# A longer written emission order, finer filler matmuls and re-measured plan durations in a linear-attention and mixture-of-experts kernel

## The chip, the cores and the metric

One core of one Trainium2 chip. The metric is the device time of one execution in microseconds (us); lower is better. The engines are PE (TensorE: matmuls, with PEld for its weight loads), DVE (VectorE), ACT (ScalarE), POOL (GpSimd) and SP (SyncE), which here only issues DMAs. Each engine works through its own instructions in the order in which the program was written; engines wait for one another through semaphores.

## What is computed

A linear attention over 8 batches, 8 heads, 576 positions and 64 dimensions, whose result goes as x (4608 rows of 512) into a dense mixture of 8 experts with Sinkhorn-normalised routing weights P.

```python
def phi(x):
    return np.where(x > 0, x, np.exp(x) - 1.0) + 1.0
kv  = einsum('bhsd,bhse->bhde', phi(k), v);  z = phi(k).sum(axis=2)
x   = einsum('bhsd,bhde->bhse', phi(q), kv) / (phi(q) @ z + 1e-06)   # (N, 512), N = 4608
logits = x @ w_gate;  P = exp(logits - logits.max())                  # (N, 8)
for _ in range(8):
    P /= P.sum(1, keepdims=True) + 1e-09
    P /= P.sum(0, keepdims=True) + 1e-09
    P *= N / E
for e in range(8):
    out += P[:, e:e+1] * (np.maximum(x @ w1[e], 0) @ w2[e])           # w1: 512x1024, w2: 1024x512
```

## The kernel before

**Stages.** In the front, the attention runs in 16 groups (8 batches by two groups of four heads), written by `att` (line 319). A group loads k, q and v; makes phi(k) with an exp on ACT and two passes on DVE (`f_e`, `f_t`, `f_m`); accumulates kv and z on PE (`f_kv`, line 366) and evicts them into a block-diagonal tile (`f_z`); transposes q on PE (`f_qt`) and makes phi(q) (`f_qe` on ACT, `f_qm` and `f_qp` on DVE); multiplies by z (`f_den`, two halves), takes the reciprocal on ACT as exp(-ln) (`f_ln`, `f_ex`); multiplies by kv (`f_num`, two halves) and writes the quotient into xT on DVE (`f_x`). All of q's, den's and the logits' results share two PSUM banks (`at2`), kv and num share one.

The experts go over nine row groups g of 512 rows each, a pair of expert and group being a unit, numbered 9e + g. Expert 0 runs beside the front and behind it: its first five groups plainly (`layer1`, line 600, four matmuls of 512 columns per block of hidden units, evicted by relu on ACT or DVE, then `f_y`, line 847, layer 2), the last four with seven products instead of eight per 2x2 block (`block7`, line 701). From unit 9 on, `unit` (line 926) does both layers with seven products: for layer 1 the products m1 to m7 of two halves a and b (`pm`, 4 matmuls of 256 columns each, evicted by `f_seed`, `f_s2`, `f_s5`, `f_h11`, `f_h21` on ACT and `f_h12`, `f_h22` on DVE), for layer 2 the products y1 to y7 (8 matmuls each). The sums of weights that these need are made on DVE once per expert, W from w1 and T from w2 (`combos`, four instructions each); the sums of h once per unit, S (`f_S`, line 933, four instructions). A product of layer 2 is scaled by P and added to acc on DVE (`f_e`, line 982, two per product), except y2, which goes over ACT (`f_a`) and POOL (`f_g`). Groups 0 to 7 of expert 0 are finished before P is known: their layer 2 is copied to acc (`f_fin`) and scaled later in place, 32 instructions of `f_s` (line 876), on DVE or ACT.

**Who sets the order.** Every piece of work is a task with an engine (or a choice of two), a planned duration, its dependencies and the buffers that it takes. `_Plan.run` (line 54) emits the tasks one by one. First it takes those of a written list, `_FRONT`, number and engine letter (p PE, a ACT, d DVE, g POOL, s SP, m a DMA's landing, n none), 993 of them, which ends on PE with unit 9's y6. From there on it always emits the task that the plan can start first, the smaller `prio` first where several can. From unit 8 on the order on PE is also a fixed chain:

```python
    order = "y1 y5 y2 a7 y6 y3 a4 b1 b5 y7 b6 b3 b2 b7 A1 A5 y4 b4 A6 A3 A2".split()
```

In a unit's stretch y stands for layer 2 of the unit before, a and b for its own layer 1, A for the next unit's half a. Each such stretch is 112 matmuls of 256 columns.

**Filler.** At the start PE has nothing to do; `f_warm` (line 537) multiplies zero tiles into a bank that nobody reads, 47 matmuls of 512 columns in 34 tasks, each put behind the one before and held by its own earliest time (`after`).

**Loads.** All loads of q, k, v and of the weights (which convert to 16 bits) are issued on POOL, in order, at most eight in flight; the first k goes over SP. Expert e's w1 comes in two halves, w2 in one piece (in quarters and halves for expert 0). From unit 9 on x is read back from DRAM per unit, on SP (`x_load`), where `x_blocks` stored it before.

Of the kernel before, what the change touches and what calls it, by code (L numbers as in the profile page):

```python
# [17 lines left out]
class _Plan:  # L18
# [119 lines left out]
    1n 2p 3p 4p 5p 6p 7p 36s 37m 8p 43d 42a 105n 94n 571n 38g 39m 0g 40g 41m 63g 64m 44d 65g 66m 67g 68m 112g 113m  # L138
    45n 9p 10p 49n 50p 114g 115m 11p 12p 51a 139g 140m 76n 46p 52d 13p 47a 14p 95g 96m 97g 98m 53d 15p 48d 141g 142m
    16p 69a 70d 17p 54p 18p 116g 117m 55a 19p 20p 71d 100g 101m 77p 72n 73p 21p 78a 79d 22p 23p 24p 56p 74a 75d 25p  # L140
    118a 80d 143g 144m 26p 57a 119d 59p 27p 102g 103m 81p 58a 28p 120d 29p 30p 166g 167m 31p 32p 82a 60d 99n 83p 106g
    107m 168g 169m 61p 62d 84a 33p 34p 125n 35p 85a 126p 86p 146d 572p 573p 127a 87d 128d 574p 88p 170g 171m 575p
    121n 109g 110m 152n 89d 145a 153p 147d 193g 194m 154a 122p 576p 129d 123a 578p 580p 155d 156d 197g 198m 124a 104n
    148n 130p 579d 577a 581d 131a 195g 196m 90g 91m 149p 132p 582p 133a 584p 150d 151d 173d 222g 223m 583a 134a 586p
    585d 137p 157p 588p 108n 138d 158a 587d 135p 172a 159p 179n 592p 590p 160a 161a 608n 92g 93m 136d 251g 252m 180p
    174d 175n 176p 181a 591d 594p 177d 589a 111n 182d 178a 249g 250m 593p 183d 162p 226g 227m 184p 595p 600a 163d
    185a 200d 253g 254m 199a 164p 186p 165d 596p 206n 609p 187a 602d 224g 225m 201d 229d 188a 305g 306m 207p 280g
    281m 202n 203p 208a 611p 204a 610d 228a 209d 210d 613p 598p 612a 278g 279m 614d 205a 211p 191p 212a 597p 213p
    192d 604d 189p 214a 615p 230d 190d 215a 220p 216p 256d 221a 599p 235n 616d 217d 255a 231n 257d 236p 237a 238d
    617p 606a 218p 311a 619p 262n 263p 219d 618a 258n 239d 232p 309g 310m 264a 233d 234d 629p 265d 621p 620a 307g  # L150
    308m 240p 259p 282g 283m 241a 260d 622a 623p 261a 266d 242p 332g 333m 243a 244a 336g 337m 624d 642p 245p 285d
    267p 641n 644p 643d 246d 268a 627p 312d 645a 269p 270a 271a 247p 291n 630p 359g 360m 248d 334g 335m 536d 292p
    313d 274p 284a 646p 275d 648p 286d 293a 272p 287n 294d 647a 628p 318n 273d 314n 361g 362m 365a 319p 537d 635d
    320a 288p 390g 391m 295d 289d 650p 290a 338a 631p 321d 296p 315p 649d 339d 297a 298p 651d 299a 652p 654p 322d
    388g 389m 316d 317d 300a 653d 303p 323p 655a 304d 632p 324a 637d 301p 366d 325p 326a 327a 656p 625p 363g 364m
    345n 302d 543d 328p 346p 657d 626p 329d 340d 347a 471g 472m 341n 330p 639a 674n 442g 443m 675p 348d 372n 331d
    367d 373p 349d 342p 374a 368n 538d 677p 469g 470m 392g 393m 343a 676a 344a 375d 660p 394a 376d 417g 418m 395d
    396d 539s 540m 350p 661p 351a 633d 679p 668a 352p 355p 353a 664p 354a 665p 544d 276p 356d 357p 358d 277a 401n
    419g 420m 402p 415g 416m 369p 545d 403a 678d 546s 547m 473g 474m 370a 658p 659p 371a 404d 377p 680a 397n 681p
    683p 666a 378a 478g 422d 526n 682d 684d 421a 379p 382p 662p 380a 381a 383d 685p 663p 687p 550d 686a 551d 448a  # L160
    423d 444g 445m 384p 689p 688a 428n 385d 429p 475a 707n 690a 405d 398p 708p 430a 431d 399a 710p 400a 406p 709a
    449d 424n 552d 553s 554m 425p 407a 555s 556m 432d 408p 426a 446g 447m 541s 542m 712p 427d 409a 711a 713d 411p
    386p 410a 714p 670d 387a 433p 412d 476d 691p 527g 528m 529g 530m 434a 450d 672a 715a 413p 414d 477d 435p 436a
    437a 716p 717d 455n 718p 548s 549m 438p 456p 557d 457a 693p 479n 439d 440p 719d 458d 694p 451n 441d 564d 565d
    459d 483n 484p 485a 452p 453a 532n 533g 534m 486d 692p 699a 720p 454d 701a 460p 461a 480p 462p 487d 481a 482d
    463a 558d 722p 467p 695p 464a 488p 468d 696p 489a 566d 465p 490p 491a 492a 466d 721a 703d 723d 697p 698p 705a
    493p 724p 494d 725p 495p 732a 730p 496d 728p 731p 738a 524n 751n 744d 745d 497p 746d 740d 747s 748m 525p 498a
    729p 741d 742d 743d 752p 796d 766p 753a 499d 754p 756p 755a 726p 957s 958m 1014s 1015m 757a 797d 758p 760p 767a
    772p 759a 773a 762p 761d 770p 500p 763d 768p 798d 764p 749s 750m 799s 800m 776p 501d 502d 765a 769a 727p 771a
    803n 804p 805a 774p 806p 808p 736a 777d 807a 810p 775d 778p 809a 535n 811a 734d 812p 503p 786p 779a 818p 813d  # L170
    504d 848d 787p 505d 849d 784p 819a 824p 794a 825a 820p 814p 821a 815d 782p 506p 828p 559d 783p 829d 816p 850d
    560s 561m 826p 507d 817a 562s 563m 790a 827d 785p 822p 792a 508d 856p 830p 823a 780p 857a 900d 781p 855n 509p
    831a 510d 834p 567s 568m 511d 835p 860p 788a 801s 802m 870p 862p 901d 836p 863a 861a 871a 842d 512p 858p 513d
    837p 859a 872p 844a 864p 514d 873a 876p 851s 852m 877a 866p 853s 854m 874p 902d 838p 867d 569s 570m 875a 903s
    904m 839p 865d 846d 878p 868p 879d 832p 869a 905s 906m 531n 515p 880p 908p 833p 909a 881d 910p 516d 911a 907n
    517d 890p 912p 882p 891p 883a 840a 914p 913a 915a 898a 922p 923a 518p 916p 884p 917d 918p 519d 919d 949d 950d
    926p 924p 925a 951d 886p 952d 928p 920p 929a 921a 885p 927a 930p 932p 960p 933d 961a 962p 892a 520d 887p 934p
    966p 948n 963a 888p 889p 967a 953d 935a 931d 896a 959n 968p 964p 965a 970p 521p 971d 936p 969d 972p 974p 976p
    522d 523d 975a 937p 977a 980p 981a 894d 973a 944a 954d 955d 982p 978p 984p 1017p 985d 1019p 986p 979a 603d 942p
    943p 706d 983d 1071s 1072m 1018a 1020a 987a 1023p 947a 988d 989d 1024a 895d 605d 940p 941p 956d 938p 601d 946d  # L180
    1025p 939p 945a 990d 1021p 992p 993a 994p 997p 1027p 669d 1016n 991d 607d 634d 1002p 1000a 996d 1022a 995d 1028d
    1001g
# [4 lines left out]
def kernel(  # L187
# [10 lines left out]
    nc = tc.nc  # L198
# [6 lines left out]
    P = 128  # L205
    PW = 64
    NJ = S // PW
    NG = N // 512
# [110 lines left out]
    def att(b, g):  # L319
# [5 lines left out]
        for nm, ten in (("k", k), ("q", q), ("v", v)):  # L325
# [15 lines left out]
            ti = fadd(("sp", 0.45) if sp else ("pool", 0.73), fn, acq=[gr, *gsw], use=gsw, prio=pr)  # L341
            tin[nm] = fadd(("dma", 1.47 if nm == "k" else 1.42), lambda _: None, deps=[ti], use=[gr, *gsw], prio=pr, lat=2.15)
# [38 lines left out]
        for r in range(2):  # L381
            def f_z(e, r=r):
                s = slice(64 * r, 64 * r + 64)
                src = gkv["tile"][s, :, 64 * r:64 * r + 2 * D].rearrange("p h (z d) -> p h z d", z=2)
                dst = gz["tile"][s, :, :, 64 * r:64 * r + 64]
                copy(e, dst, src if r == 0 else src[:, :, ::-1])
            tz.append(fadd({"dve": 0.40, "act": 0.42}, f_z, deps=[tkv, *tz], use=[gkv, gz], prio=pr))
# [70 lines left out]
    def logits(b2):  # L458
# [11 lines left out]
        t1 = lg_pe[b2] = add(("pe", 1.0), f_l, deps=wg_done + [xt_done[(b, c)] for b in (2 * b2, 2 * b2 + 1) for c in range(NDT)],  # L470
# [4 lines left out]
    def sinkhorn():  # L475
# [10 lines left out]
        for it in range(8):  # L486
# [27 lines left out]
            a = add(("dve", 2.6), f_a, deps=last, prio=-200.0)  # L514
            c = add(("pe", 0.2), f_c, deps=[a], acq=[gc], prio=-200.0, lat=0.15)
            last = [add(("dve", 0.45), f_d, deps=[c], use=[gc], prio=-200.0)]
# [18 lines left out]
    t_id[0] = add(("pool", 1.5), f_init, prio=-290.0)  # L535

    def f_warm(_, n=1):
        for _ in range(n):
            nc.tensor.matmul(yw[0], lhsT=warm[:, 0:P], rhs=warm, start=True, stop=True)
# [6 lines left out]
    for i in range(34):  # L546
        twa = add(("pe", 0.3), lambda e, n=2 if 4 <= i < 17 else 1: f_warm(e, n), deps=[twa], use=[gyw], prio=900.0, after=1.2 + 0.5 * i)
# [93 lines left out]
    def x_blocks(g):  # L641
# [10 lines left out]
        for i in range(3):  # L652
# [16 lines left out]
            last = add(("dve", 0.8 if i == 0 else 0.42), f_T,  # L669
# [8 lines left out]
        def f_st(_):  # L678
            nc.sync.dma_start(out=xd[g][:, 1536:NXB], in_=gt_["tile"].rearrange("p i c t -> p (i c t)"))
        ti = add(("sp", 0.45), f_st, deps=[last], use=[gt_], prio=0.0)  # L680
        out_ = [add(("dma", 1.5), lambda _: None, deps=[ti], use=[gt_], prio=0.0, lat=2.6)]
        ti = add(("sp", 0.9), f_raw, deps=deps + [ti], prio=0.0)
        out_.append(add(("dma", 1.0), lambda _: None, deps=[ti], prio=0.0, lat=2.6))
        x_users.append(out_[1])
        if early:
# [415 lines left out]
```

## Time and profile before

| | us |
|---|---|
| median of 3 runs (lowest, highest) | 970.96 (970.43, 971.53) |
| profiled execution | 971.46 |
| its span, first to last instruction | 969.7 |
| PE busy in it | 956.1 |
| DVE, ACT, POOL busy | 769.4, 572.1, 144.1 |
| granted TensorE clock, mean | 0.999 |
| first zero matmul starts | 1.33 |
| first transposes, first kv, first den start | 6.91, 9.37, 12.38 |
| first expert matmul starts | 21.76 |
| first layer-2 product of units 9, 10, 11, 12 | 199.06, 212.13, 226.72, 238.94 |

The parts of the page are read so: busy time of each engine; the same in 40 slices; DMA queues; the chain of work that ended last; the costliest groups of instructions, each with its line, shapes, count, busy time and the idle time before it, with what ended that idle time; the DMA issues. A matmul's end is modelled and includes its drain, so that matmuls that follow each other overlap in the record: the distance of their starts is what one costs.

### The profile page before, as it was taken

The numbers are of one execution on the slowest core, as the hardware profiler recorded it, in microseconds if no ns is written. First come the engines' busy times: TensorE is split into PE (matmuls) and PEld (weight loads), VectorE is DVE, ScalarE is ACT, GpSimd is POOL, SyncE is SP. The second block draws the span as 40 slices with busy tenths as digits, with TensorE's granted clock in tenths as the row PEclk, the third lists the DMA queues.
The fourth block names the chain that finished last, engine by engine and source line by source line (L and its number), as shares of the span: only waits on it lengthen the run. The fifth ranks groups of instructions, "written<-read, shape, count | busy, mean of one in ns | idle before, by whom it ended". The sixth has DMA issues, their size and how long they took to land.

```text
span 969.7 us, 21145 instructions
## 1 busy us (share of the span) xinstructions
PE 956.1 (99%) x8625; PEld 795.5 (82%) x8625; DVE 769.4 (79%) x1469; ACT 572.1 (59%) x1016; POOL 144.1 (15%) x209
## 2 busy tenths in 40 slices
PE   8999999999999999999999999999999999999998
PEld 4555566678888888888888888888888888888886
DVE  6887888797887888878887888878887888877775
ACT  6787864575555555555555555555555555555553
POOL 6422100020112111111112111111112111111110
PEclk9999999999999999999999999999999999999999
DMA  9998854062226322272226322272226322235554
GB/s 219 253 202 213 148 174 169 4 153 85 77 76 129 108 76 74 74 161 74 72 72 138 100 74 75 76 163 76 77 76 139 102 78 76 77 99 164 163 164 109
DMA packets 46193, 112.52 MB, mean 116 GB/s; under 512 B 4368, under 2 KB 26640, under 8 KB 46096
## 3 DMA queue, kind: packets, MB, share of 16 engines
q1 hardware_dynamic: 21056, 75.57, 23.8%
q0 software_dynamic: 24640, 35.07, 19.4%
q8 instruction: 67, 1.10, 0.5%
q10 hardware_dynamic: 400, 0.52, 0.2%
q14 instruction: 30, 0.25, 0.1%
HBM read 119.69 MB, written 17.69 MB: 142 GB/s over the span
## 4 chain that ended last, share of the span: by engine, by line
PE 89%; DVE 5%; DMA 3%; ACT 2%; issue 1%; POOL 0%; DVEq 0%; ACTq 0%; POOLq 0%
PE ye L969 33%; PE hq L745 23%; PE att L745 12%; PE Zye L745 6%; PE Zye L969 5%; PE ye L851 5%; DMA kin<-in_k_dram 2%; PE hq L623 1%; DVE h L780 1%; DMA vv<-in_v_dram 1%; DVE xT L449 1%; PE kv_ps L371 1%; PE att L398 0%; DVE qpT L405 0%; PE att L421 0%
## 5 line engine op out<-in xcount | busy, mean ns | idle before, releaser
L983 DVE SCALAR_TENSOR_TENSOR acc<-ye,P_sb,acc 128x256 f32<-128x256 f32 x620 | 267.2, 480 | 127.4 <-PE ye L969 126.7
L745 PEld LDWEIGHTS <-W 128*128 128x128 f16 x2144 | 209.8, 98 | 29.0 <-issue 2.3
L969 PEld LDWEIGHTS <-S 128*128 128x128 f16 x1984 | 194.0, 98 | 25.0 <-DVE S L942 2.6
L993 POOL TENSOR_TENSOR acc<-acc,st 128x256 f32<-128x256 f32 x124 | 87.6, 726 | 710.1 <-ACT st L990 665.3
L969 PE MATMUL ye<-T,S 128*128 128x256 f16 x1488 | 192.8, 273 | 0.1
L745 PEld LDWEIGHTS <-w 128*128 128x128 f16 x1608 | 157.3, 98 | 21.7 <-issue 1.4
L777 ACT ACTIVATE h<-hq 128x512 f16<-128x512 f32 x134 | 80.1, 598 | 148.8 <-PE hq L745 146.3
L969 PEld LDWEIGHTS <-h 128*128 128x128 f16 x1488 | 145.6, 98 | 16.8
L745 PE MATMUL att<-xs,W 128*128 128x256 f16 x1008 | 151.2, 273 | 0.7 <-DVE h L780 0.7
L745 PE MATMUL hq<-xs,W 128*128 128x256 f16 x1008 | 151.2, 273 | 0.1
L745 PE MATMUL hq<-xs,w 128*128 128x256 f16 x1008 | 140.9, 273 | 0.7 <-DVE h L780 0.7
L774 ACT ACTIVATE h<-Zye 128x512 f16<-128x512 f32 x134 | 80.1, 598 | 40.5 <-PE Zye L745 40.5
L990 ACT ACTIVATE st<-Zye,P_sb 128x256 f32<-128x256 f32 x124 | 52.1, 470 | 76.8 <-PE Zye L969 76.8
L780 DVE CUSTOM_DVE_ANT_0 h<-att,s 128x512 f16<-128x512 f32 x126 | 86.7, 688 | 11.1 <-ACT s L764 10.8
L942 DVE TENSOR_TENSOR S<-h 128x1024 f16<-128x1024 f16 x124 | 85.5, 689 | 12.5 <-ACT h L777 12.5
L764 ACT COPY s<-hq 128x512 f32<-128x512 f32 x126 | 73.4, 582 | 36.7 <-PE hq L745 36.7
L757 ACT COPY Zye<-hq 128x512 f32<-128x512 f32 x134 | 77.9, 581 | 23.8 <-PE hq L745 23.6
L780 DVE CUSTOM_DVE_ANT_0 h<-hq,s 128x512 f16<-128x512 f32 x126 | 86.8, 688 | 2.2 <-PE att L504 1.7
L851 PE MATMUL ye<-w,h 128*128 128x512 f16 x312 | 77.0, 379 | 0.6 <-DMA w<-in_moe_w_dram 0.6
L745 PE MATMUL Zye<-xs,w 128*128 128x256 f16 x504 | 75.6, 273 | 0.0
L771 ACT COPY s<-att 128x512 f32<-128x512 f32 x126 | 74.5, 591 | 1.2 <-DVE h L780 1.2
L969 PE MATMUL ye<-w,S 128*128 128x256 f16 x496 | 64.3, 273 | 1.9 <-DVE S L942 1.9
(102 smaller groups left out, 946.0 us busy)
## 6 DMA issues: line engine op xcount, KB each, us to landing
xs<-xd SPq DMA_DIRECT2D x63, 896.0 KB, 4.6
kin<-in_k_dram POOLq DMA_DIRECT2D x15, 576.0 KB, 9.1
out_dram<-acc SPq DMA_DIRECT2D x67, 128.0 KB, 2.4
w<-in_moe_w_dram POOLq DMA_DIRECT2D x16, 512.0 KB, 8.3
w<-in_moe_w_dram POOLq DMA_DIRECT2D x7, 1024.0 KB, 14.3
qin<-in_q_dram POOLq DMA_DIRECT2D x16, 288.0 KB, 8.4
vv<-in_v_dram POOLq DMA_DIRECT2D x16, 288.0 KB, 8.7
xd<-acc SPq DMA_DIRECT2D x5, 512.0 KB, 6.5
```

What stands on the lines that cost most here:

```text
L745: nc.tensor.matmul(dst[:, p, :], lhsT=lhs(p, c), rhs=rhs(c), start=(first and p == 0 and c == 0), stop=(c == 1), skip_group_check=True)
L757: nc.scalar.copy(out=Zt[1], in_=gX["tile"])
L764: nc.scalar.copy(out=gs2["tile"], in_=gX["tile"])
L771: nc.scalar.copy(out=gs5["tile"], in_=gR["tile"])
L774: nc.scalar.activation(out=hd(0, 0), in_=Zt[1], func=AF.Relu)
L777: nc.scalar.activation(out=hd(1, 0), in_=gX["tile"], func=AF.Relu)
L780: nc.vector._custom_dve(TENSOR_ADD_SAT, out=dst, in0=ps, in1=sb, s0=3.0e38, s1=0.0)
L851: nc.tensor.matmul(gy[tt]["tile"], lhsT=gh["tile"][:, f, ds(P * tt, P)], rhs=gw2["tile"][:, f, :], start=(f == 0), stop=(f == NFT - 1))
L942: nc.vector.tensor_tensor(out=Sx[:, i], in0=a0, in1=a1, op=op)
L969: nc.tensor.matmul(bank(g_)[:, s, :], lhsT=lhs(s, kk), rhs=rhs(kk), start=(new and s == 0 and kk == 0), stop=(kk == 3), skip_group_check=True)
L983: nc.vector.scalar_tensor_tensor(out=dst(), in0=bank(g_)[:, s, :], scalar=P_sb[:, gg, e:e + 1], in1=dst(), op0=ALU.mult, op1=ALU.add)
L993: nc.gpsimd.tensor_tensor(out=dst(), in0=dst(), in1=gst["tile"], op=ALU.add)
```

## The change

1. `_FRONT` is replaced: 1201 tasks in place of 993. All four compute engines' order and that of the loads differ from the first lines on, and the list now ends on PE with unit 12's y7, in unit 13's stretch, instead of unit 9's y6.
2. The zero matmuls are 46 tasks of one each (before: 34 tasks with 47), with earliest times 0.25 us apart.
3. Planned durations and earliest times of some tasks are other numbers. They emit nothing themselves; they enter where the planner chooses, that is, behind the written list.

The order of instructions on each engine in the two built programs, where the prediction speaks of it:

- PE: the chain from unit 9's layer 2 on is the same. Twenty zero matmuls stand ahead of the first transposes (14 before) and three between the first kv and the first den (ten before).
- DVE, from the first S of unit 9 to the first S of unit 10: before 15 of the 32 `f_s` and one W of expert 2; now 3 `f_s` and no W. Behind the written list, in unit 12 and 13, five `f_s` and all four W of expert 2 stand together, the four W between the second `f_h22` of unit 13 and its first S. From the evictions behind unit 13's last S on, the order is the same as before.
- ACT: 14 `f_s` before, 12 now. 19 of the 36 copies of expert 0's layer 2 (24 before), the others on DVE.
- POOL: one half of the gate weights is loaded first of all; the identity is made behind seven loads instead of one; the loads of expert 2's w1 and w2 stand behind the adds of unit 11 (before: among those of unit 9).

```diff
 _FRONT = """
-    1n 2p 3p 4p 5p 6p 7p 36s 37m 8p 43d 42a 105n 94n 571n 38g 39m 0g 40g 41m 63g 64m 44d 65g 66m 67g 68m 112g 113m
...
-    1001g
+    1n 2p 3p 4p 5p 102g 103m 6p 7p 8p 9p 10p 11p 12p 13p 14p 15p 16p 17p 18p 19p 20p 21p 117n 48s 49m 50g 51m 52g 53m
...
+    1217a
 """
...
-            ti = fadd(("sp", 0.45) if sp else ("pool", 0.73), fn, acq=[gr, *gsw], use=gsw, prio=pr)
-            tin[nm] = fadd(("dma", 1.47 if nm == "k" else 1.42), lambda _: None, deps=[ti], use=[gr, *gsw], prio=pr, lat=2.15)
+            ti = fadd(("sp", 0.45) if sp else ("pool", 0.73), fn, acq=[gr, *gsw], use=gsw, prio=pr, after=0.74 if sp else 1.75)
+            tin[nm] = fadd(("dma", 1.47 if nm == "k" else 1.42 if n else 2.3), lambda _: None, deps=[ti], use=[gr, *gsw], prio=pr, lat=2.15)
...
-            tz.append(fadd({"dve": 0.40, "act": 0.42}, f_z, deps=[tkv, *tz], use=[gkv, gz], prio=pr))
+            tz.append(fadd({"dve": 0.43, "act": 0.37}, f_z, deps=[tkv, *tz], use=[gkv, gz], prio=pr))
...
-            a = add(("dve", 2.6), f_a, deps=last, prio=-200.0)
-            c = add(("pe", 0.2), f_c, deps=[a], acq=[gc], prio=-200.0, lat=0.15)
-            last = [add(("dve", 0.45), f_d, deps=[c], use=[gc], prio=-200.0)]
+            a = add(("dve", 2.29 if it == 0 else 2.78), f_a, deps=last, prio=-200.0)
+            c = add(("pe", 0.112), f_c, deps=[a], acq=[gc], prio=-200.0, lat=0.1)
+            last = [add(("dve", 0.41), f_d, deps=[c], use=[gc], prio=-200.0)]
...
-    t_id[0] = add(("pool", 1.5), f_init, prio=-290.0)
-
-    def f_warm(_, n=1):
-        for _ in range(n):
-            nc.tensor.matmul(yw[0], lhsT=warm[:, 0:P], rhs=warm, start=True, stop=True)
+    t_id[0] = add(("pool", 0.6), f_init, prio=-290.0, after=1.75)
+
+    def f_warm(_):
+        nc.tensor.matmul(yw[0], lhsT=warm[:, 0:P], rhs=warm, start=True, stop=True)
...
-    for i in range(34):
-        twa = add(("pe", 0.3), lambda e, n=2 if 4 <= i < 17 else 1: f_warm(e, n), deps=[twa], use=[gyw], prio=900.0, after=1.2 + 0.5 * i)
+    for i in range(46):
+        twa = add(("pe", 0.43 if i < 9 else 0.215), f_warm, deps=[twa], use=[gyw], prio=900.0, after=1.2 + 0.25 * i)
...
-        out_ = [add(("dma", 1.5), lambda _: None, deps=[ti], use=[gt_], prio=0.0, lat=2.6)]
-        ti = add(("sp", 0.9), f_raw, deps=deps + [ti], prio=0.0)
-        out_.append(add(("dma", 1.0), lambda _: None, deps=[ti], prio=0.0, lat=2.6))
+        out_ = [add(("dma", 2.3), lambda _: None, deps=[ti], use=[gt_], prio=0.0, lat=2.6)]
+        ti = add(("sp", 1.3), f_raw, deps=deps + [ti], prio=0.0)
+        out_.append(add(("dma", 2.6), lambda _: None, deps=[ti], prio=0.0, lat=2.6))
...
-                    fin_prev[(gg, dh)] = add(("pool", 0.8), f_g, deps=[t, fin_prev[(gg, dh)]], use=[gst],
+                    fin_prev[(gg, dh)] = add(("pool", 0.74), f_g, deps=[t, fin_prev[(gg, dh)]], use=[gst],
```

## The prediction

> **What bounds the kernel now.** I read the page's busy times first, then the stages, then who ended TensorE's (PE's) waits, then the two engines' order of time around the longest wait.
>
> ```profile
> span 969.7 us, 21145 instructions
> PE 956.1 (99%) x8625; PEld 795.5 (82%) x8625; DVE 769.4 (79%) x1469; ACT 572.1 (59%) x1016; POOL 144.1 (15%) x209
> ```
>
> ```profile
> 0.00:21.76 21.76, 18.76 (x151) 9.19 (x152) 12.59 (x21) 12.70 (x15) 14.07 (x26) 1.00 1.02 221
> 21.76:38.20 16.44, 15.68 (x151) 8.64 (x149) 13.76 (x22) 13.02 (x18) 7.12 (x11) 1.00 1.19 240
> 38.20:129.20 91.00, 88.68 (x858) 50.00 (x857) 72.49 (x121) 72.83 (x100) 22.31 (x32) 1.00 0.88 190
> 129.20:199.00 69.80, 68.86 (x506) 46.55 (x505) 57.47 (x128) 36.61 (x69) 0.00 (x0) 1.00 0.35 120
> 199.00:222.00 23.00, 20.69 (x184) 17.54 (x182) 19.65 (x43) 18.93 (x35) 4.95 (x7) 1.00 0.68 132
> ...
> 234.20:940.00 705.80, 705.80 (x6467) 632.63 (x6466) 566.23 (x1086) 400.73 (x751) 92.13 (x130) 1.00 0.35 100
> ```
>
> The second fence is a table of stages; a row gives window, length, and busy time (with counts) of PE, weight loads, DVE, ACT, POOL. PE is the bound, and from 234 to 940 us it never idles: nothing there can pay. What can move lies before 222 us. PE idles 2.3 us in 38 to 129, 0.9 in 129 to 199, 2.3 in 199 to 222. Each real stall costs some 0.16 more than its idle time, because a 256-column matmul is counted 0.273 us long but the next starts after 0.109 (the chain of waits has 16 of them in 1.75). The first 21.8 us are latency, filled with zero matmuls.
>
> ```profile
> PE ye L969 <- DVE S L942: 1.9, 1, 1.9
> PE hq L623 <- DVE h L630: 1.4, 2, 1.0
> ...
> PE kv_ps L371 <- DMA vv<-in_v_dram: 0.8, 1, 0.8
> ...
> PE ye L851 <- DMA w<-in_moe_w_dram: 0.6, 1, 0.6
> ```
>
> Except for the two DMA rows, an engine's queue is late, DVE's above all. The longest wait, in order of time on DVE:
>
> ```profile
> 209.54 1.27 DVE L880 TENSOR_SCALAR acc<-acc,P_sb 128x512 f32<-128x512 f32 x3
> 210.72 0.87 DVE L983 SCALAR_TENSOR_TENSOR acc<-ye,P_sb,acc 128x256 f32<-128x256 f32 x2
> 211.51 0.48 DVE L880 TENSOR_SCALAR acc<-acc,P_sb 128x512 f32<-128x512 f32 x1
> 211.94 0.69 DVE L909 TENSOR_TENSOR W<-w 128x1024 f16<-128x1024 f16 x1
> ...
> 217.52 0.83 DVE L942 TENSOR_TENSOR S<-h,S 128x1024 f16<-128x1024 f16 x1
> ```
>
> DVE runs without a pause into the fourth S of unit 10, for which PE stands still from 216.53 to 218.41. The deferred scalings of acc (L880) were put ahead of it.
>
> **The hand-over, units 9 and 10.** On PE, unit 9's first layer-2 matmul starts at 199.06, unit 10's at 212.13, unit 11's at 226.72; a steady unit takes 12.23 (238.94 to 251.17). Excess: 0.84 + 2.36 = 3.2 us. In the old instruction order 15 scalings and one W stand on DVE between unit 9's first S and unit 10's. Starts follow each other by 0.60 for S, h and W, 0.40 for scalings and evictions. Ten evictions, four S and four h make 4.0 + 2.4 + 2.4 = 8.8; 15 x 0.40 + 0.6 more is 15.4, over the 12.23. In the new order 3 scalings and no W stand there: 10.0, so it fits, and one or two in the two units behind. Following the new queues through units 9 to 12 against PE's blocks (0.87 for eight matmuls, 0.44 for four), each S, h and eviction ends before its reader, the tightest by 0.1 to 0.3. I take 0.3 of 3.2 as left: **-2.9** (between -3.2 and, if the tight places slip in each unit, -1.5).
>
> **What it costs two units later.** The written order now ends in unit 12, and what it did not place comes at once behind it: on DVE 3 scalings, 2 evictions, a scaling, two h, then W, scaling, W, eviction, W, eviction, W, and only then the S of unit 13. Before, the W's came one per unit. With unit 13's layer 2 due at 251.17 in the old clock: four evictions end at 245.35 (one h stands between them), three scalings 246.55, evictions 247.35, scaling 247.75, two h 248.95, then 4 x 0.60 + 0.40 + 2 x 0.40 = 3.6 gives 252.55, and S ends at 253.2. It ended at 251.4. The matmul that reads it was due at 252.05: late by 1.25. In this unit two evictions and an h also stand before the third and fourth S, the evictions wait for the late matmul (ends 254.35), and the fourth S ends at 257.05 for a reader due at 255.11 + 1.25: 0.75 more. **+2.0.** Least: 3.8 us of extra work (3 W, 5 scalings) less the 2.3 that DVE idles in such a unit and 0.5 of lead, 1.0; most: nothing hidden, 3.8. From the evictions after this fourth S on, DVE's order is the old one, ACT's and PE's likewise in the units around it, so the loss is paid once.
>
> **The start.** One zero matmul fewer (46 for 47). On POOL one of the gate-weight loads now stands ahead of the first q (its issue 0.69, its transfer 0.2 in the landing times) and the identity behind seven issues, ready near 7.6. Twenty zero matmuls stand before the first transposes (14 before): 11 at 0.43, nine at 0.22, to 7.8; the transposes ran at 6.91. What is gained: only three, not ten, zero matmuls then stand between the first kv and the first den, which ran at 12.38 behind 2.3 us of them (they are on the chain of waits); eviction of kv behind the second pass of q gives about 11.9. Carried on through exp, Ln and the two xT, the first hq starts between 0.9 earlier and 0.6 later than 21.76. But this start is not what counts at 38 us: layer 2 waits there for the second half of w2, which landed at 37.28. The same transfers stand ahead of it in the queue, plus 0.2. In the new order a den and a num (0.49) are done before that wait. So by 38 us: **-0.1**, from -0.5 to +0.6.
>
> The slow zero matmuls are 0.43 apart in this trace, 11 of them. [...]
>
> **38 to 199 us.** Old stalls with their 0.16: 2.3 idle and some five gaps, 3.1 us, to 129; 0.9 and five gaps, 1.7 us, to 199. The switches to transposes and kv (0.09 to 0.14 each at their edges) stay: both orders have 54. Between den and den, and from transposes to den, the new order leaves PE as much other work as the old one (1.16 us or more, 3.6 or more, past the start), so no new chain stands out. Nor is any longer: But DVE gets fuller: from the last xT (129.2) to unit 9's first S (194.6) it was busy 53.1 of 65.4 us (81%). The new order puts seven more acc copies (0.60), seven scalings (0.40) and three other instructions (some 0.6) there, 62 us, while PE's work up to that S grows to some 70 us: 88%. No view shows the waits of an order that has not run. Bounds: all 4.8 gone, or 3 us of new ones. I take half of the first and 40% of the second as gone, -1.5 and -0.7: **-2.2**.
>
> On SP the load of unit 10's x stands behind more stores; it was issued at 132 and first read at 190.7, which hides it. Planned durations emit no instruction.
>
> **Sum.** -0.1 - 2.2 - 2.9 + 2.0 = -3.2. The profiled execution took 971.46 (span 969.7 and 1.8 around it); the median of the runs is 970.96, 0.5 lower. 970.96 - 3.2 = **967.8**.
>
> **Rivals.**
> The pile-up is absorbed: if DVE runs ahead in unit 12, the W's fall into its idle 1.31 and 0.46 us and the term is 0.5: 966.3; with every stall to 199 gone too, 963.7. For it: 2.3 us idle per unit. Against: three scalings already stand in the 1.31. Chance 0.18.
>
> The middle keeps its stalls: other gaps replace the old ones, +0.5 for -2.2, and 970.5. For it: the old order also was written out there and has 4.8 us of stalls; DVE is at 88%. Against: each old wait has one late producer, and moving it is cheap. Chance 0.22. If the new order gives the gain back in unit 13 too (3.8), 972.3.
>
> Slower: DVE waits for expert 2's w1. Its loads now stand on POOL behind the adds of unit 11, whose second ACT part stands behind six other ACT operations: issue near 236.2 and 236.9 (203.2 and 204.6 before). The first W is reached on DVE near 248.95. If the second half takes over 12.0 us to land, all of DVE's queue stops, S and evictions behind it and PE behind those, 1 us for 1 us. Weight loads landed after 5.8 to 18.5, median 11.1: at 18.5, 6.5 us late, 967.8 + 6.5 = 974.3. It decides above 14: net no gain; over 17 and it is slower by more than 0.2%. Against it: the same two halves took 5.8 and 7.3. Chance 0.10.
>
> **How the numbers follow.** Forecast 0.50, rivals 0.18, 0.22 and 0.10. Each term's ends together are less likely than one of them: 964.0 to 972.5 holds 8 in 10. A measurement here tells 0.2%, 1.9 us, from no change: under 969.0 is faster. Of the forecast 0.45 of the 0.50 lies there, all of the first rival: 0.63. Within: 0.05, most of the second and a little of the third: 0.24. Slower: 0.13.
>
> **What would show it.** Layer-2 starts of units 9, 10, 11 12.3 apart; one unit, 12 to 13, some 14.2 long with W four times before S on DVE; first den before 12.38; steady units of 12.23. I am wrong if the 38 to 199 stage idles over 3.2 us, or if DVE waits for w before W.

## The result, and the profile after

The changed kernel is slower: 981.16 us median (979.57 to 982.0, 4 executions) beside 971.01 for the kernel before on the same chip, a ratio of 1.0103 with a 95% interval of 1.0085 to 1.012. Measured again later beside other kernels it took 980.23 (978.03 to 981.19, 5 executions), ratio 1.0087 (1.0073 to 1.0102). The prediction was 967.8, and its range ended at 972.5.

The page of the changed kernel, span and busy times:

```profile
span 977.8 us, 21138 instructions
...
PE 959.2 (98%) x8624; PEld 796.0 (81%) x8624; DVE 774.7 (79%) x1481; ACT 566.0 (58%) x1004; POOL 145.2 (15%) x209
```

The span is 8.1 us longer than before, and PE is busy only 3.1 us longer. The stages of the changed kernel, in the columns of the table shown before (window, length, PE, weight loads, DVE, ACT, POOL busy, granted clock, DMA share, GB/s):

```profile
38.20:129.20 91.00, 88.70 (x889) 50.24 (x887) 75.37 (x127) 71.60 (x96) 22.48 (x31) 1.00 0.84 186
129.20:199.00 69.80, 64.18 (x417) 40.98 (x416) 53.59 (x123) 31.12 (x57) 0.00 (x0) 0.98 0.35 112
199.00:222.00 23.00, 21.62 (x189) 18.21 (x188) 17.71 (x34) 13.95 (x26) 1.41 (x2) 1.00 0.20 67
...
262.00:940.00 678.00, 677.31 (x6205) 606.85 (x6204) 542.51 (x1042) 383.49 (x720) 90.23 (x127) 1.00 0.35 100
```

From 129 to 199 us PE idles 5.6 us where it idled 0.9, and DVE, which was to become fuller there, is emptier: 53.6 busy where it was 57.5. So this looks less like an engine with too much to do than like engines that wait for each other; the experiments test it. The mean clock of the stage is 0.98, so something slowed PE even while it worked.

Since the orders differ, a start alone tells little. The next table gives time lost: the start of an instruction less the work that PE had done by then, at the distances at which PE's instructions follow each other without a wait (0.109 us for 256 columns, 0.216 for 512), zero matmuls not counted.

| start of | before | after | two tiles, own order of before | two tiles, new order |
|---|---|---|---|---|
| first expert matmul (21.5 us) | 16.57 | 16.34 | 16.54 | 16.44 |
| layer 2 of expert 0's group 0 (38.7) | 18.11 | 18.17 | 18.14 | 18.25 |
| the zero matmuls that end the front (131) | 23.92 | 23.91 | 22.98 | 23.98 |
| first layer-2 product of unit 9 | 26.61 | 34.68 | 24.07 | 24.62 |
| of unit 12 | 29.74 | 35.72 | 27.06 | 24.54 |
| of unit 14 | 29.69 | 37.71 | 27.00 | 26.68 |

(The last two columns belong to experiments below.) In the changed kernel the front loses what it lost, the stage of the Sinkhorn 10.8 us instead of 2.7, the hand-over from unit 9 to unit 12 1.0 instead of 3.1, unit 13 2.0 instead of nothing. From there on both run alike.

Who ended PE's waits in the changed kernel:

```profile
PE att L515 <- DVE gs L510: 3.3, 1, 3.3
PE att L515 <- DVE h L790: 1.6, 2, 1.4
PE kv_ps L382 <- DMA vv<-in_v_dram: 1.5, 2, 1.2
...
PE ye L979 <- DVE S L952: 0.9, 2, 0.7
PE att L755 <- DVE h L790: 0.8, 1, 0.8
```

The longest wait is that of a column sum of the Sinkhorn loop (`f_c`, L515): 3.3 us for the row pass on DVE (`f_a`, whose last instruction writes gs, L510). An iteration is a ring: `f_a` on DVE (2.8 us), `f_c` on PE, `f_d` on DVE (`Dc`, L522), and the next `f_a`. PE around this wait, in order of time:

```profile
168.62 0.39 PE L515 MATMUL att<-gs,ones_t 128*128 128x8 f32 x2 [1.39 <-DVE h L790]
...
172.32 0.60 PE L755 MATMUL att<-xst,W 128*128 128x256 f16 x4
176.21 0.39 PE L515 MATMUL att<-gs,ones_t 128*128 128x8 f32 x2 [3.28 <-DVE gs L510]
...
177.73 1.91 PE L861 MATMUL ye<-w,h 128*128 128x512 f16 x4
```

and DVE:

```profile
167.88 0.68 DVE L790 CUSTOM_DVE_ANT_0 h<-att,acc 128x512 f16<-128x512 f32 x1
172.96 0.16 DVE L522 SCALAR_TENSOR_TENSOR Dc<-Dc,att 128x8 f32<-128x8 f32 x1 [4.40 <-PE att L755]
...
175.70 0.45 DVE L510 TENSOR_REDUCE gs<-wt 128x8 f32<-128x288 f32 x1
...
181.01 0.16 DVE L522 SCALAR_TENSOR_TENSOR Dc<-Dc,att 128x8 f32<-128x8 f32 x1 [3.66 <-PE att L755]
```

The column sum of iteration 5 was done at 169.01. The `f_d` that reads it started at 172.96, after 4.40 us in which DVE did nothing, and what released it was not the column sum (L515) but a product of layer 1 (L755), m5 of unit 8, that ended at 172.92. `f_d` has no use for m5. One iteration later the same again, 3.66 us. The built program says why. With the instruction's number in the program, its engine and what it touches (att+0 and att+256 are the first bank, att+512 the second):

```
3526 PE  f_c, iteration 5   writes att+512        waits for DVE count 250 (3524)
3524 DVE h12 of unit 7      reads  att+0
3572-3578 PE  m5 of unit 8  writes att+0, att+256   3578 raises PE to 1462
3579 DVE f_d, iteration 5   reads  att+512        waits for PE count 1462 (3578)
```

Both banks are one tile, `at2` (the program calls it att). In both waits listed here, that of `f_c` for h12 and that of `f_d` for m5, the wait covers an access of another engine to the other bank, because it was written ahead in the same tile. The planner counts two banks that are free of each other. In the new order `f_d` of iteration 5 is written behind m5 of unit 8, so it waits for m5, which itself comes up on PE only at 172.32, and `f_a` and the next `f_c` wait behind it.

Over the whole stage, from 129 to 200 us, `f_d`'s waits in the changed kernel are

```profile
DVE Dc L522 <- PE att L755: 8.6, 3, 4.4
DVE Dc L522 <- ACT acc L781: 2.9, 3, 1.2
```

none of them for a column sum. This could have been read in the kernel before. There the first row of DVE's waits in the same stage is

```profile
DVE Dc L511 <- PE att L745: 2.9, 4, 1.0
```

Four of its eight `f_d` were released by a product (L745) and not by their column sum (L504): up to 1.0 us each, with other work on PE to cover it.

### The profile page after: what moved, and what is told of

Read it like the earlier page. It is cut to its first block, busy times and chain, and to the rows that moved or that the text cites. A ratio compares the mean times of both kernels' runs of the same rounds, so it can differ in the third digit from the quotient of the medians.

```text
span 977.8 us, 21138 instructions
## 1 busy us (share of the span) xinstructions
PE 959.2 (98%) x8624; PEld 796.0 (81%) x8624; DVE 774.7 (79%) x1481; ACT 566.0 (58%) x1004; POOL 145.2 (15%) x209
## 4 chain that ended last, share of the span: by engine, by line
PE 87%; DVE 6%; DMA 4%; ACT 1%; issue 1%; POOL 1%; DVEq 0%; ACTq 0%; POOLq 0%
PE ye L979 32%; PE hq L755 23%; PE att L755 12%; PE Zye L755 6%; PE Zye L979 5%; PE ye L861 4%; DMA vv<-in_v_dram 2%; PE hq L633 2%; DMA w<-in_moe_w_dram 1%; DVE h L790 1%; DMA qin<-in_q_dram 1%; PE kv_ps L382 1%; PE att L409 1%; PE num_ps L432 0%; DVE W L919 0%
## 5 line engine op out<-in xcount | busy, mean ns | idle before, releaser
L755 PEld LDWEIGHTS <-W 128*128 128x128 f16 x2144 | 209.9, 98 | 29.7 <-issue 2.8
L755 PEld LDWEIGHTS <-w 128*128 128x128 f16 x1608 | 157.7, 98 | 22.8 <-issue 2.8
L755 PE MATMUL att<-xs,W 128*128 128x256 f16 x1008 | 151.2, 273 | 0.9 <-DVE h L790 0.8
L755 PE MATMUL hq<-xs,W 128*128 128x256 f16 x1008 | 151.2, 273 | 0.0
L755 PE MATMUL hq<-xs,w 128*128 128x256 f16 x1008 | 140.9, 273 | 0.9 <-DVE h L790 0.9
L755 PE MATMUL Zye<-xs,w 128*128 128x256 f16 x504 | 75.6, 273 | 0.0
```

What stands on the lines that cost most here:

```text
L755: nc.tensor.matmul(dst[:, p, :], lhsT=lhs(p, c), rhs=rhs(c), start=(first and p == 0 and c == 0), stop=(c == 1), skip_group_check=True)
```

## The experiments

The kernel before, measured anew beside each group of these runs, took 971.40, 971.61 and 970.56 us; the ratios are to it. Differences to the changed kernel are taken from the 980.23 us of its second measurement.

**`f_d` written earlier, all queues kept.** `_FRONT` with three tokens moved (the letter is the engine, d DVE, p PE); the order within each engine is unchanged:

```diff
-    527p 920p 856a 894p 844p 895a 851p 845p 922p 858a 528d 529d
-    530p 852d 921a 926p 924p 927a 898p 923a 934p 928p
...
-    961d 531d 940p
+    527p 528d 920p 856a 894p 844p 895a 851p 845p 922p 858a 529d
+    530p 852d 961d 531d 921a 926p 924p 927a 898p 923a 934p 928p
...
+    940p
```

(527p and 530p are `f_c` of iterations 5 and 6, 528d and 531d their `f_d`, 922p and 928p products m5 and m3, 961d a W.)

> The changed kernel, with the order of every engine's own queue kept to the instruction. Only the place at which two instructions of VectorE are written among those of the other engines differs: the normalisation f_d of Sinkhorn iterations 5 and 6 (with expert 1's first W ahead of the latter) is written right behind its column sum f_c, instead of behind the product m5 (and m3) of unit 8 that writes the other bank of the same PSUM tile. Theory A (a wait counts what was written before it: in the changed kernel f_d waits for m5, which it doesn't need, since both banks are one tile): f_d of iteration 5 starts within 0.4 us of its column sum's end at 169.0 and not at 172.96; TensorE's idle stretch of 3.28 us and the half clock of 3.41 us behind it (1.7 us of time) go; 976 us (974.5 to 977.5) beside 981.2. Theory B (VectorE has too much work in this stage, and the order of its queue makes the Sinkhorn late): nothing in its queue is changed, so the idle stretch stays; 981 us, within 0.5.

Measured: 974.63 us (973.9 to 975.38), ratio 1.0031 (1.0019 to 1.0044), 5.6 us less than the changed kernel. DVE:

```profile
168.97 0.16 DVE L520 SCALAR_TENSOR_TENSOR Dc<-Dc,att 128x8 f32<-128x8 f32 x1 [0.48 <-PE att L513]
```

`f_d` starts at 168.97 and not at 172.96, released now by its column sum (L513 here). On PE the next column sum follows m5 (172.24) without a wait:

```profile
172.68 0.29 PE L513 MATMUL att<-gs,ones_t 128*128 128x8 f32 x2
```

With every queue as it was, a load of DVE that is too high cannot be the cause: theory B is out for this wait. Still there is the wait of 1.39 us ahead of iteration 5's column sum.

**Two tiles in place of one, in the changed kernel and in the kernel before.** When the front ends, the tile of two banks is closed and two tiles of one bank are opened; no queue changes:

```diff
+        aps_st.close()
+        ap1 = ctx.enter_context(tc.tile_pool(name="ap1", bufs=1, space=PSUM))
+        at1.extend(ap1.tile([P, 512], FP32, tag=f"at{i}", name=f"at{i}") for i in range(2))
...
-        return at2[:, (len(p_att["order"]) - 1) % 2]
+        i = (len(p_att["order"]) - 1) % 2
+        return at1[i] if at1 else at2[:, i]
```

> The changed kernel with the PSUM tile of two banks closed where the front ends and two tiles of one bank opened in its place; every queue keeps its order. Theory A: the column sum of iteration 5 no longer waits 1.55 us for the addition h12 that reads the other bank, none of the eight f_d waits for a product or a copy of the other bank, and the 3.28 us of idle time with the 1.7 us of half clock go: of the 10.8 us lost in this stage some 3 stay, 973 us (971 to 975.5), below the run with f_d written earlier. Theory B (load of VectorE): 981 us, within 0.5.

> The same two tiles in the kernel before, with its own order. It loses 2.7 us in this stage. Theory A: its f_d wait for products of the other bank too (up to 1 us of VectorE's idle time each), but with cover; 970.4 us (969.5 to 971.0). If the two tiles were worth something by themselves, whatever the order, it would gain as much as the changed kernel does (5 us or more): 966 or less.

Measured: the changed kernel with two tiles 968.38 us (967.58 to 969.88), ratio 0.9968 (0.9956 to 0.9979); the kernel before with two tiles 968.88 (968.51 to 969.76), ratio 0.9973 (0.9962 to 0.9985). Both are below the expected ranges: the first fell by 11.9 us, the second by 2.5. The changed kernel with two tiles, two stages of the table:

```profile
129.20:199.00 69.80, 69.80 (x494) 47.91 (x491) 60.66 (x137) 36.89 (x68) 0.00 (x0) 1.00 0.37 121
199.00:222.00 23.00, 23.00 (x213) 20.61 (x212) 18.84 (x39) 15.24 (x29) 2.87 (x4) 1.00 0.19 59
```

PE waits for nothing from 129 to 222 us, with DVE at 60.66 of 69.80, 87%. The first is lower than expected because 3 us of the stage's loss had been left in place that also came from the tile: 0.6 is left (24.62 - 23.98), and the wait of PE for `h` of 0.6 us in the hand-over went too. In this run accesses of two engines to the two banks overlap. DVE reads its column sum in one bank, 0.16 us from 155.45, while PE writes a product into the other, 0.60 us from 155.27 (the program gives the column sum the second tile and the product the first):

```profile
155.45 0.16 DVE L525 SCALAR_TENSOR_TENSOR Dc<-Dc,at 128x8 f32<-128x8 f32 x1
```

```profile
155.27 0.60 PE L761 MATMUL at<-xst,W 128*128 128x256 f16 x4
```

In the kernel before, the run with two tiles is 2.5 us faster, but only part of that is the tiles'. By the traces 0.94 of the lost time goes at 98 us, in the front, where the two programs are still the same: a load of k came 0.9 us earlier in that execution. In the Sinkhorn the two tiles pay 1.6 (2.7 to 1.1); the hand-over keeps its 3.0. So the tile costs the old order little and the new one much (10.1 by the same table); it is the meeting of the tile with this order that the change brought.

**The W of expert 2, one in a unit.**

```diff
-            tW = add(("dve", 0.685), f_W, deps=tw1 + [t_close, tW, pe_id.get((NG * (e - 1) + i + 1, "b22"))], acq=[gW] if i == 0 else [], use=[gw1, gW],
+            tW = add(("dve", 0.685), f_W, deps=tw1 + [t_close, tW, pe_id.get((NG * (e - 1) + i + (4 if e == 2 else 1), "b22"))], acq=[gW] if i == 0 else [], use=[gw1, gW],
```

> The changed kernel with one dependence changed: the four W of expert 2 wait for units 13 to 16 instead of 10 to 13, so that behind the end of the written order they come one in a unit and not all in unit 13. The stage of the Sinkhorn is left as it is. Pile-up theory: the 2.0 us that unit 13 loses to its VectorE work (waits of 0.53, 0.33 and 0.85 us among them) go almost whole: 979.4 us (978.8 to 980.2) beside 981.2. Rival (the four W need 2.7 us of VectorE wherever they stand, and VectorE sets the pace here): the loss only moves to units 14 to 16, 981 within 0.5.

Measured: 978.24 us (977.75 to 979.64), ratio 1.0072 (1.006 to 1.0085), 2.0 below the changed kernel, and by the trace 1.8 (lost at unit 14: 35.88 for 37.71). (The time is under the expected range because that was taken from the first measurement, 981.2; the same holds for the loads of v below.) The rows of DVE in unit 13 of the changed kernel show the bunch as the prediction had it:

```profile
254.86 0.68 DVE L919 TENSOR_TENSOR W<-w 128x1024 f16<-128x1024 f16 x1
...
255.86 0.68 DVE L919 TENSOR_TENSOR W<-W,w 128x1024 f16<-128x1024 f16 x1
...
256.86 0.68 DVE L919 TENSOR_TENSOR W<-w 128x1024 f16<-128x1024 f16 x1
...
257.85 0.68 DVE L919 TENSOR_TENSOR W<-w,W 128x1024 f16<-128x1024 f16 x1
258.45 0.68 DVE L952 TENSOR_TENSOR S<-h 128x1024 f16<-128x1024 f16 x1
```

With the W spread PE waits nowhere between 244 and 272 us. The units behind had the room, so the loss did not move on to them: the rival is out.

**Zero matmuls in the long gap.** 12, and in another run 2, ahead of column sum 6, into the column sum's own bank:

```diff
             def f_c(_, it=it, gc=gc):
                 gc["tile"] = att_bank()[:, 0:E]
+                for _i in range(12 if it == 6 else 0):
+                    nc.tensor.matmul(att_bank(), lhsT=warm[:, 0:P], rhs=warm, start=True, stop=True)
```

> The changed kernel with 12 zero matmuls (128x512, about 0.215 us each at full clock) written into the column sum's own bank ahead of column sum 6, where TensorE stood idle for 3.28 us until 176.2; nothing is taken away and nothing else is moved. The column sum still waits for VectorE's gs at 176.15, so the 3.28 us stay lost. Clock theory (the half clock of 3.41 us behind the gap follows from the idle stretch): no stretch of half clock there, the products behind column sum 6 take their usual times and 1.7 us come back, 979.4 us (978.8 to 980.2) beside 981.2. Rival (the products behind it are slow for a reason of their own, or the zero matmuls delay the column sum by more than they save): 981 or more.

> As the run with 12 zero matmuls ahead of column sum 6, but with 2: TensorE is busy for about 0.45 us after f_d of iteration 5 at 173.4 and then idle for about 2.4 us instead of 3.28. If the half clock needs an idle stretch of nearly 3.28 us: clock 1.0 behind it, 979.3 us. If an idle stretch of 2.4 us is enough: half clock for about 3.4 us again, 981 us. The gap of 1.39 us ahead of column sum 5 left the clock at 1.0 in the changed kernel's trace.

Measured: with 12, 978.90 us (977.94 to 979.1), ratio 1.0077 (1.0065 to 1.0089), 1.3 below the changed kernel by the median and 1.6 by the spans (976.2 for 977.8). The stretch ahead of and behind the column sum, changed kernel first (a row is one stretch; the third number from the right is the granted clock):

```profile
173.46:176.87 3.41, 0.66 (x6) 0.63 (x7) 3.24 (x8) 0.00 (x0) 0.00 (x0) 1.00 0.00 0
176.87:180.28 3.41, 3.41 (x14) 1.81 (x13) 0.48 (x1) 1.58 (x3) 0.00 (x0) 0.50 0.02 5
```

and the run with 12:

```profile
176.30:180.30 4.00, 4.00 (x30) 2.84 (x31) 1.92 (x6) 2.15 (x4) 0.00 (x0) 1.00 0.02 4
```

30 matmuls in 4.00 us, and 14 in 3.41 in the changed kernel: behind the gap PE's granted clock was 0.50, and in the run with 12, where PE was kept busy, 1.00. From the column sum to m3 of unit 8 it is 4.08 us in the changed kernel and 2.42 with 12 zero matmuls, 1.66 of the loss. With 2, the idle stretch is 2.44 us and the half clock came all the same (0.50 from 177.76 to 181.18; 979.69 us, one execution). So an idle stretch of nearly 3.28 us was not needed here.

**The loads of v.** `404g` (v of group 12) and `375g` (v of group 11) exchange their places, with their landings:

```diff
-    361d 354p 386a 404g 405m 355a 645a 668p
+    361d 354p 386a 375g 376m 355a 645a 668p
...
-    456g 457m 651a 375g 376m 686n 672p 379d
+    456g 457m 651a 404g 405m 686n 672p 379d
```

> The changed kernel with two loads of POOL's queue exchanged: of the two loads of v that stand about q's at 81.1 to 83.3 us, the one that TensorE waited for at 89.71 (1.16 us, kv_ps <- DMA vv) is issued first, the other one last. Theory (the stretch from 38 to 129 us gained nothing because this wait for a transfer took the place of the stalls that went): the wait of 1.16 us goes, no other of its size comes, 980.1 us (979.7 to 980.5). Rival (the transfers share one rate there, and the other load of v is now late): a wait of the same size at the next kv product, at about 95 us; 981 to 981.5.

Measured: 978.57 us (977.34 to 978.89), ratio 1.0074 (1.0062 to 1.0086); 1.7 below the changed kernel by the median; by the trace 1.04 less is lost by the end of the front (22.87 for 23.91). Of the two waits of kv for v after 38 us (1.5 us) one of 0.4 is left:

```profile
PE kv_ps L380 <- DMA vv<-in_v_dram: 0.4, 1, 0.4
```

The load that PE needed first had been issued third of three, at 82.58 us, and landed at 90.8. The rival's second wait did not come.

**The mends together.** Two tiles and the W spread; then the loads of v as well.

> The changed kernel with both mends that gave time by themselves: two tiles of one bank from the end of the front on, and the four W of expert 2 one in a unit. If the two are independent: 968.4 - 1.9 = 966.5 us (965.9 to 967.2). If the earlier Sinkhorn had already made the room that the W need in unit 13: 968.4, no change from two tiles alone. The kernel before with two tiles stands at 968.9; the written order is worth the difference to it.

> As the kernel with two tiles and the W spread, with the two loads of v exchanged as well. If all three are independent: 965.4 us (964.7 to 966.2). If the exchange only moves the wait: 966.5.

Measured: 967.42 us (966.18 to 968.04), ratio 0.9962 (0.9949 to 0.9974); and 965.46 (965.39 to 966.04), ratio 0.9943 (0.9931 to 0.9955). By the spans the W are worth 1.9 (966.7 to 964.8), the loads 1.2 more (963.6); the medians of the first pair, which were not measured side by side, differ by 1.0 only, and the first lies 0.2 above its range. By the traces the three add up. The last is faster than both kernels, 3.4 us below the kernel before with two tiles: that much the new order is worth without its three mishaps. Here too PE is never idle from 129 to 222 us.

**The three mends without the second tile.** The two `f_d` earlier, the W spread, the loads exchanged.

> The changed kernel with its one tile of two banks, and the three mends that need no other tile: f_d of iterations 5 and 6 written right behind their column sums, the W of expert 2 one in a unit, the loads of v exchanged. If the mends are independent: 974.6 - 1.9 - 1.1 = 971.6 us (970.8 to 972.5), no faster than the kernel before; what is then left to the 965.5 us of the kernel with two tiles (some 6 us) is the price of the other waits between the banks, in this stage and the hand-over. If the one long stall were all that the single tile costs: 967 us or less.

Measured: 971.69 us (971.21 to 972.09), ratio 1.0007 (0.9998 to 1.0016), as summed up. Left to two tiles are 6.2 us. In this run PE still waits 1.6 us for `h` ahead of column sums, 0.8 for `h` shortly before unit 9's layer 2 and 0.6 in the hand-over, all of which two tiles removed.

**Twelve zero matmuls fewer**, in the fastest kernel:

```diff
-    def f_warm(_):
-        nc.tensor.matmul(yw[0], lhsT=warm[:, 0:P], rhs=warm, start=True, stop=True)
+    def f_warm(_, i=0):
+        if i < 34:
+            nc.tensor.matmul(yw[0], lhsT=warm[:, 0:P], rhs=warm, start=True, stop=True)
```

> The fastest kernel so far (two tiles, W spread, loads of v exchanged; 965.5 us), with the last 12 of the 46 zero matmuls left out; they compute nothing that is used. It tells what the change's 12 further zero matmuls are worth. Theory of the prediction (they lie in idle time of TensorE before 18 us, worth 0.1 us): 965.5 us, within 0.5. Rival (without them the idle time there lets the clock fall again, as the idle stretch ahead of column sum 6 did): half clock for 3.4 us about 20 us from the start, 967 us or more.

Measured: 965.47 us (965.24 to 965.71), no change, and yet the rival's mechanism came:

```profile
15.99:19.40 3.41, 1.33 (x7) 0.51 (x6) 2.27 (x4) 3.40 (x4) 1.42 (x3) 1.00 1.17 227
19.40:22.82 3.42, 3.19 (x24) 1.69 (x24) 2.47 (x4) 2.62 (x3) 1.40 (x2) 0.50 1.15 235
```

The clock fell for 3.41 us at 19.4, and not in this execution alone: the five show a mean granted clock of 0.997 or 0.998, those of the fastest kernel 0.999 or 1.000. A num product there starts 1.1 us later (24.13 for 23.01), but at 37.85 against 37.65 only 0.2 is left: in the fastest kernel PE waits for transfers in between (0.43 us for v at 26.9, 0.16 for w at 37.5), and here it doesn't. So the half clock cost almost nothing here: waits for transfers that were there anyway took up most of it.

**The changed kernel again.**

> The changed kernel as it is, once more, beside the others of this call: the four measurements of its first run (979.6 to 982.0 us) are the base that the single mends are taken from, and two of the mends gave 1 us more by the median than by their traces. All theories: 980.5 us (979.5 to 981.5); if the first run was high by itself, at the lower end.

Measured: 980.23 us, as said. In this trace the same gap of 3.28 us brought 6.83 us of half clock and not 3.41.

## Why the prediction was wrong

The steps, with the profiled execution 8.1 us above that of before:

- **What bounds it.** Right: PE, with nothing to gain behind the hand-over. From 262 to 940 us PE is busy 677.31 of 678.
- **The start, -0.1 to 38 us.** Measured +0.06. The first den came at 12.11 (11.9 predicted), and the loads absorbed the rest, as the prediction said of w2.
- **38 to 129 us, -1.5.** Measured -0.07 in lost time. The old stalls for `h` did go; one wait of 1.16 us for a load of v took their place, and exchanging two loads gave 1.0 back. The prediction looked at PE's and DVE's order and not at the order of the loads on POOL. It also misread the largest of the old stalls, PE's 1.0 us for `h` at 98 us: DVE was late there not by its queue, but because it had stood idle for 3.94 us for a load of k. In the other trace of the same instructions (the kernel before with two tiles) k came 0.9 us earlier and this stall isn't there. So some of the 1.5 to be gained was chance of that execution.
- **129 to 199 us, -0.7: the step that failed.** Measured +8.1 up to unit 9's layer 2. The prediction's own sign of being wrong, over 3.2 us of idle time from 38 to 199, came: 7.9. The prediction sized this stage by DVE's load (88%) and, as "No view shows the waits of an order that has not run", bounded it with "3 us of new ones". The load was right and harmless (87% with two tiles, no wait of PE). What it left out, and so put at nothing, is that here a wait on the shared tile covered what was written ahead of it in either bank; an order moves such waits even where every queue's own order is sound. `f_d` waited 8.6 us for products; 3.3 us of that became idle time of PE at one place, 1.7 more came from the half clock that followed, 1.4 from a column sum that waited for the other bank's reader, and the rest from smaller waits: with two tiles all of it went.
- **The hand-over, -2.9.** Measured -2.1 from unit 9 to unit 12 (lost 1.04 for 3.13). The mechanism, the scalings that no longer stand ahead of S, is right. Most of the 1.0 that was left hangs on the shared tile too (a wait of 0.6 us for `h`): with two tiles PE waits for nothing there, -3.2 against the kernel before.
- **Unit 13, +2.0.** Measured +2.0 (lost 35.72 to 37.71 from unit 12 to 14), by the instructions named; spreading the W gave 1.8 of it back. The size is better than its working: the loss is spread over two starts (unit 12 to 13 took 13.05 us, 13 to 14 took 13.44, where 14.2 was forecast for the first), and PE's first wait, 0.37 us, is for an eviction and not for S. So the close match of the sum is in part luck.
- **The rivals.** None was the case. DVE never waited for expert 2's w1. The middle that "keeps its stalls" had the right stage, at a price (970.5 to 972.3) from the same bound, which was too narrow.

With every step at its measured size, the sum is 0.06 - 0.07 + 8.1 - 2.1 + 2.0 = 8.0 of the 8.1. The step that failed makes up 8.8 of the 11.3 between forecast and measured change of the profiled execution, the missing gain from 38 to 129 us another 1.4.

## What to carry to other kernels

Before trusting an order, ask of each wait what it covers: here a tile of two independent banks made `f_d` wait 4.40 us for a product in the other bank, and `f_c` 1.39 us for `h`, because these were written ahead in the same tile. A reader that is released by an instruction whose result it does not read (`Dc` by L745 and not by L504) shows this in the profile of the kernel before. Give separately used banks separate tiles, then reorder; a planner that counts the banks as independent otherwise moves the cost to where it can't see it. When a written order is made longer, look also at what it leaves to the first unit behind its end, and at the order of loads among themselves.

## What the runs showed of the hardware

In the changed kernel's trace the granted clock was 1.00 from 6.21 to 176.87 us, 0.50 for the next 3.41 us and 1.00 again from 180.28 on; in its second trace it was 0.50 for 6.83 us. In the 3.41 us ahead of a fall PE was idle in part only, by the profile's busy times: 2.75 us in the changed kernel's trace, 2.65 in its second one, 1.94 in the run with 2 zero matmuls and 2.08 in the run with 34 at the start. With 1.73 us of idle time in 3.41 (1.68 busy) the clock stayed at 1.00 in the kernel before with two tiles:

```profile
213.42:216.83 3.41, 1.68 (x16) 1.27 (x14) 2.27 (x6) 2.07 (x4) 1.54 (x2) 1.00 0.97 257
216.83:220.24 3.41, 3.41 (x34) 3.06 (x32) 1.93 (x5) 2.19 (x4) 0.00 (x0) 1.00 0.00 0
```

These are five traces; how much idle time brings a fall in general they do not show. The gap of 3.28 us did not cost the same in both traces of the changed kernel. In the first, PE was busy for all of the 3.41 us at half clock, and the clock behind them was 1.00. In the second, the first 3.41 us at half clock still held 0.63 us of idle time (2.78 busy), and the half clock went on for 3.42 more:

```profile
175.93:179.34 3.41, 2.78 (x12) 1.91 (x13) 1.74 (x4) 1.28 (x3) 0.00 (x0) 0.50 0.00 0
179.34:182.76 3.42, 3.42 (x13) 1.81 (x12) 0.33 (x2) 0.86 (x2) 0.00 (x0) 0.50 0.02 5
```

What decides between the two is not shown. The scatter of the changed kernel's times goes with this clock. Of its nine executions the two with a mean granted clock of 1.000 took 978.0 and 978.3 us, the one at 0.998 took 979.6, those at 0.997 and 0.996 took 980.2 to 981.2, and the one at 0.994 took 982.0. So in some executions the gap seems to have cost no half clock at all, and even those are 7 us or so slower than the kernel before; where the half clock lay is known only for the two that were profiled.
